# Bias rows for attention: the 16 queries of a set four apart over both halves of the partitions, in two transfers a set

## The chip, the cores and the metric

One core of a Trainium2 chip runs the whole program. The metric is its device time in microseconds; the time of a kernel is the median of its runs. The work is spread over TensorE (PE), VectorE (DVE), ScalarE (ACT), GpSimd (POOL) and the SyncE queue (SP), which here issues every transfer to 16 DMA engines. A profile shows one execution.

## What is computed

Attention with a bias that depends on the positions, and then two feed-forward networks, over B = 4, H = 8, S = 576, D = 64:

```
scores = q @ k.T / sqrt(D)
psi_rel = log1p(abs(i - j));  psi_i = log1p(max(i, 1))
bias[h, i, j] = relu((psi_rel / psi_i) * w1 + b1) @ w2[:, h]      # 32 hidden units
attn = softmax(scores + bias) @ v                                  # 2304 x 512 when laid out
x = max(attn @ w1m, attn @ w2m, attn @ w3m) @ w_out                # hidden width 768
out = g(x @ w_in) @ w_out2                                         # hidden width 2048
```

The bias is the same for all four batches: a table of 8 heads x 576 queries x 576 keys.

## The kernel before, in words

The 576 queries are cut into blocks j = 0 to 3 of 128 queries and a block SJ = 4 of 64. A slot is one head (for SJ, two heads) of one block and one batch. For each slot TensorE makes scores (line 543), VectorE adds the bias and finds the maximum (line 552), ScalarE takes the exponential (line 554) and a 16-bit high half (line 570), GpSimd the low half (lines 571 and 572); the transfer of line 574 transposes both, and TensorE multiplies with v (line 594). In block 0 every other slot is transposed by TensorE. Beside the attention run the first network (lines 649 to 671), whose results go to DRAM (line 678), and the decoding of all weights, which come as 64-bit integers (lines 329, 341 to 344, 155 and 156). The second network (lines 867 and 891) fills the end, from about 700 us.

The bias of a block lies in a table `bias_sb[j]`, [128 queries, 8 heads, 576 keys], which line 552 reads with queries on partitions. It is made in sets of 16 queries, eight sets a block (four for SJ). For a set r, `bias_relu` makes four tiles m (c = 0 to 3). The 128 partitions of a tile hold 4 groups g of 32 hidden units; all groups read one window of the precomputed table `rel`, in which group g is shifted by its own g, and add a column of `tq`. So one tile covers four neighbouring queries, 32j·4 + 16r + 4c + g. `bias_rows` multiplies the tiles with `coef` on TensorE (line 308), which gives 128 rows, row 32c + 8g + h for head h; ScalarE scales each row by a column of `ips` (line 311); and one transfer moves the 128 rows to 16 neighbouring partitions of the table:

```
last_bias[0] = SP.dma_start(bias_sb[j][16 * r:16 * r + 16], t)
```

In block SJ eight small transfers a set, one for each head, do this (line 316).

The eight sets of block 0 are made first, in the order r = 0, 4, 2, 6, 1, 5, 3, 7 (line 725); the loads of lines 730 to 736 are held behind the last of them. The sets of blocks 1 to 3 and SJ are spread over the slots of the block before. The code says in which order work is wanted (priorities, the `sooner` contexts, the counts in `PRM`), and a scheduler that simulates the kernel fixes the order of instructions on each engine when it is built. SP works through its queue in that order: a transfer waits for what it moves, and all behind it wait too.

The last stores are those of line 910, in block SJ two transfers to `out`, whose destination counts 2 batches, 64 rows and 512 columns.

Of the kernel before, what the change touches and what calls it, by code (L numbers as in the profile page):

```python
# [13 lines left out]
ALU = mybir.AluOpType  # L14
# [6 lines left out]
def kernel(ctx: ExitStack, tc: tile.TileContext, qt, kt, vr, small, mw1, mw2, mw3, mwo, win, wo2, out):  # L21
# [7 lines left out]
    V, A, G, T, SP = nc.vector, nc.scalar, nc.gpsimd, nc.tensor, nc.sync  # L29
    P = 128  # L30
    B, H, S, D = 4, 8, 576, 64
# [60 lines left out]
    def st(shape, dt, tag):  # L92
        return sb.tile(shape, dt, tag=tag, name=tag, bufs=BUFS.get(tag, 1))
# [16 lines left out]
    def newcol(n=1):  # L110
        c = col[0]
        col[0] += n
        return vec[:, c:c + n]

    wm = aw.rearrange("p (f i s k c) -> p f i s k c", f=NF1, i=3, s=2, k=KK)
    bias_sb = [ab[:, j % 2].rearrange("p (h k) -> p h k", h=H) for j in range(4)] + [ws[:, 3072:3072 + 4 * S].bitcast(F32).rearrange("p (h k) -> p h k", h=4)]
# [6 lines left out]
    BLK = [(128 * i, 128, 512) for i in range(4)] + [(512, 64, 256)]  # L123
    SJ = 4
# [5 lines left out]
    MAGIC = 12582912.0  # L130
# [31 lines left out]
    if True:  # L162
# [4 lines left out]
        G.memset(ones, 1.0)  # L167
        c_half = newcol()
        G.memset(c_half, 0.5)
        c_g, c_gm, c_p, c_o = newcol(), newcol(), newcol(), newcol()  # L170
        for g in range(4):
            G.memset(c_g[32 * g:32 * g + 32], float(g))
            G.memset(c_gm[32 * g:32 * g + 32], -float(g))


        RW0 = 575
        rel = st([P, 1152], F32, "rel")
        REL = (slice(464, 1152), slice(0, 464))
        pc = st([P, 180], F32, "pc")
        tq, ips = pc[:, 0:144], pc[:, 144:180]  # L180
# [2 lines left out]
        w1c, b1c, w2c = sm[:, 0:1], sm[:, 1:2], sm[:, 2:10]  # L183

        def iota(t, step, n, base, per=0):
            G.iota(t, pattern=[[step, n]], base=base, channel_multiplier=per, allow_small_or_imprecise_dtypes=True)

        iota(rel[:, REL[0]], 1, 688, 464 - RW0)
        iota(tq, 4, 144, 0)
        iota(c_p, 1, 1, 0, 1)  # L190
        iota(ips, 16, 36, 0)
        iota(ident, 1, P, 0, -1)
        iota(rel[:, REL[1]], 1, 464, -RW0)

# [10 lines left out]

        V.tensor_scalar(c_o, c_p, 0.125, -0.4375, ALU.mult, ALU.add)
        V.tensor_scalar(c_o, c_o, MAGIC, None, ALU.add)
        V.tensor_scalar(c_o, c_o, -MAGIC, None, ALU.add)
        V.tensor_scalar(tq, tq, c_g, 1.0, ALU.add, ALU.max)
        V.tensor_scalar(ips, ips, c_o, 1.0, ALU.add, ALU.max)  # L210
        A.activation(rel[:, REL[0]], rel[:, REL[0]], AF.Abs, bias=c_gm)
        A.activation(rel[:, REL[0]], rel[:, REL[0]], AF.Ln, bias=1.0)
        A.activation(pc, pc, AF.Ln, bias=1.0)
# [69 lines left out]
        last_bias = [None, None]  # L283
# [5 lines left out]
        def bias_relu(j, r, engs, tag):  # L289

            ms = []
            for c in range(4):
                x = 32 * j + 4 * r + c
                m = st([P, 9, P], F16, tag).rearrange("p c k -> p (c k)").bitcast(F32) if tag == "pt" else st([P, S], F32, tag)
                win_ = rel[:, RW0 - 4 * x:RW0 - 4 * x + S]
                if engs[c] == "v":
                    V.tensor_scalar(m, win_, tq[:, x:x + 1], 0.0, ALU.add, ALU.max)  # L297
                else:
                    A.activation(m, win_, AF.Relu, bias=tq[:, x:x + 1])
                ms.append(m)  # L300
            return ms

        def bias_rows(j, r, ms, tag):

            pb = ps.tile([P, 2, 512], F32, tag="s", name="s", bufs=2)
            for a in range(2):
                for c in range(4):
                    T.matmul(pb[32 * c:32 * c + 32, a, :288], (coefp if j == SJ else coef), ms[c][:, 288 * a:288 * a + 288], start=True, stop=True)  # L308
            t = st([P, 2 * S], F16, tag).bitcast(F32) if tag == "phl" else st([P, S], F32, tag)
            x = 8 * j + r  # L310
            last_bias[1] = A.activation(halves(t), pb[:, :, :288], AF.Copy, scale=ips[:, x:x + 1])
            if j != SJ:
                last_bias[0] = SP.dma_start(bias_sb[j][16 * r:16 * r + 16], t)
            else:
                for h in range(H):
                    SP.dma_start(bias_sb[j][64 * (h // 4) + 16 * r:64 * (h // 4) + 16 * r + 16, h % 4], t[h:P:8])  # L316


        cnt = {"r": 0, "b": 0}
# [195 lines left out]
        def prefetch(i):  # L515

            if i >= NS:
                return
            u, s = slots[i]
            if u.j == SJ and i + PRM["sa"] < NS:  # L520
                v = slots[i + PRM["sa"]][0]
                load(("q", v.j, v.b, v.x))
            load(("q", u.j, u.b, u.x))
            load(("k", min(u.j, 3), u.b, s if u.j == SJ else s // 2))
# [197 lines left out]
        v_load(0)  # L722
        moe_load(0)
        conv_left = list(range(NF1))
        for x, r in enumerate((0, 4, 2, 6, 1, 5, 3, 7)):
            bias_rows(0, r, bias_relu(0, r, PRM["b0"], ("m", "pt")[x % 2]), ("sp", "phl")[x % 2])
            if x == 1:
                prefetch(1)
        with tc.issue_after(last_bias[0].ins):
            prefetch(2)  # L730
            prefetch(4)
            prefetch(6)
            for ft in range(1, 5):
                moe_load(ft)
                if ft == 2:
                    v_load(1)
# [178 lines left out]
        for x in range(len(work) + GL):  # L915
            if x < len(work):
                y, ft = work[x]
# [9 lines left out]
            if x >= GL:  # L927
                y, ft = work[x - GL]
                size = GROUP if y == 0 else NF2
                g = ft // size if y == 0 else 3 + y  # L930
# [41 lines left out]
```

## Time and profile before

| | |
|---|---|
| median of 3 runs | 1101.57 us (1098.8 to 1102.5) |
| the profiled execution | 1101.92 us |
| its span | 1100.1 us |
| busy: PE, DVE, ACT, POOL | 975.6, 652.2, 562.3, 267.9 us |
| transfers by share of 16 engines | 60.6% of the span |

Busy times are sums over the span, and they don't say which engine ends a stretch. The transfers fill the DMA engines in the first two thirds and hardly appear after; TensorE is busy nearly throughout, and without gaps from 700 us on. A share of the DMA engines over 1 comes from packets that overlap on an engine. [...]

### The profile page before, as it was taken

What the parts mean: (1) busy time and instruction counts of PE and PEld (TensorE: products, weight loads), DVE (VectorE), ACT (ScalarE), POOL (GpSimd) and SP (SyncE); (2) the same over time, 40 slices, a digit from 0 to 9 for tenths busy, and PEclk for the clock granted to TensorE, in tenths of its full rate; (3) what the DMA queues carried; (4) which work ended last, traced back from release to release, by engine and by line L of the source; (5) the groups of instructions that cost most, each with busy time, mean ns of one, the idle gap of its engine ahead of it and who ended that gap; (6) DMA issues with size and microseconds to landing.
All of it is one profiled execution on the core that took longest, in us unless ns stands there. A gap on an engine that the chain in (4) does not pass through costs nothing.

```text
span 1100.1 us, 21901 instructions
## 1 busy us (share of the span) xinstructions
PE 975.6 (89%) x8497; PEld 638.4 (58%) x8497; DVE 652.2 (59%) x1516; ACT 562.3 (51%) x1097; POOL 267.9 (24%) x372
## 2 busy tenths in 40 slices
PE   7457788899899998899899778899999999999994
PEld 4244467676677776677687657644444444444462
DVE  6588784686346773455565587876664454454452
ACT  8685574665465654566676555642332242242341
POOL 0212132554455552635566110100000000000000
PEclk9576698799999998999999999999999999999998
DMA  8997999899999995999999845110020010010010
GB/s 187 267 254 183 243 203 171 178 206 227 214 230 214 217 179 136 224 192 218 183 226 178 206 140 163 58 39 1 1 77 1 1 58 1 1 39 1 1 40 19
DMA packets 233291, 147.84 MB, mean 134 GB/s; under 512 B 177764, under 2 KB 207972, under 8 KB 232676
## 3 DMA queue, kind: packets, MB, share of 16 engines
q1 hardware_dynamic: 233188, 146.45, 60.6%
q8 instruction: 66, 1.08, 0.4%
q14 instruction: 37, 0.30, 0.1%
HBM read 78.65 MB, written 14.68 MB: 85 GB/s over the span
## 4 chain that ended last, share of the span: by engine, by line
PE 55%; DMA 20%; DVE 8%; ACT 6%; issue 4%; SPq 4%; POOL 2%; DVEq 0%; ACTq 0%; POOLq 0%
PE pm L867 17%; PE s L891 17%; PE pm L649 9%; DMA pt<-phl 8%; PE s L543 5%; PE pav L594 3%; PE s L308 2%; DMA v<-in_moe_w_out_dram 2%; DMA ws<-in_moe_w_out_dram 2%; ACT sp L554 2%; SPq L316 1%; DMA x_d<-hl 1%; DMA xT<-phl 1%; POOL phl L572 1%; DVE sp L552 1%
## 5 line engine op out<-in xcount | busy, mean ns | idle before, releaser
L649 PE MATMUL pm<-xT,aw 128*128 128x256 f16 (+1 forms) x2160 | 246.2, 269 | 22.9 <-ACT hm L654 11.3
L649 PEld LDWEIGHTS <-aw 128*128 128x128 f16 x2160 | 193.2, 100 | 70.8 <-issue 47.3
L572 POOL TENSOR_TENSOR phl<-sp,phl 128x512 f16<-128x512 f32 x128 | 157.2, 1228 | 0.0
L543 PE MATMUL s<-k,qz 64*128 64x288 f32 (+1 forms) x576 | 136.5, 472 | 21.2 <-DVE mx L552 17.3
L554 ACT ACTIVATE sp<-sp,mx 128x576 f32<-128x576 f32 x144 | 110.5, 768 | 71.6 <-DVE mx L552 70.7
L891 PEld LDWEIGHTS <-phl 128*128 128x128 f16 x864 | 84.5, 98 | 98.3 <-DVE phl L883 0.2
L552 DVE CUSTOM_DVE_ANT_0 sp<-s,ab 128x576 f32<-128x576 f32 x128 | 93.3, 752 | 53.5 <-PE s L543 30.9
L879 DVE SCALAR_TENSOR_TENSOR sp<-pm,vec,sp 128x512 f32<-128x512 f32 (+1 forms) x80 | 55.8, 697 | 112.7 <-ACT sp L878 112.7
L878 ACT ACTIVATE sp<-pm,vec 128x512 f32<-128x512 f32 (+1 forms) x80 | 58.7, 733 | 123.8 <-PE pm L867 122.2
L891 PE MATMUL s<-ab,phl 128*128 128x512 f16 x486 | 112.5, 379 | 0.0
L882 ACT ACTIVATE phl<-sp,vec 128x512 f16<-128x512 f32 (+1 forms) x80 | 54.3, 678 | 109.5 <-DVE sp L880 109.5
L543 PEld LDWEIGHTS s<-k,qz 64*128 64x128 f32 (+1 forms) x576 | 74.5, 205 | 47.4 <-DVE mx L552 20.7
L570 ACT ACTIVATE phl<-sp 128x576 f16<-128x576 f32 x128 | 85.4, 674 | 28.8 <-DMA pt<-phl 22.9
L571 POOL TENSOR_TENSOR phl<-sp,phl 128x64 f16<-128x64 f32 x128 | 45.4, 355 | 215.1 <-ACT phl L570 202.9
L297 DVE TENSOR_SCALAR m<-rel,pc 128x576 f32<-128x576 f32 x124 | 81.6, 717 | 25.6 <-PE s L308 25.6
L594 PEld LDWEIGHTS <-pt 128*128 128x128 f16 x1792 | 74.5, 101 | 33.7 <-DMA pt<-phl 14.8
L883 DVE SCALAR_TENSOR_TENSOR phl<-sp,vec,phl 128x512 f16<-128x512 f32 (+1 forms) x80 | 55.8, 698 | 51.7 <-ACT phl L882 51.6
L594 PE MATMUL pav<-v,pt 128*128 128x64 f16 x1568 | 70.3, 197 | 17.4 <-DMA pt<-phl 11.4
L671 PE MATMUL pm<-hh,wo 128*128 128x256 f16 x648 | 80.4, 279 | 5.8 <-DVE hm L656 2.5
L867 PEld LDWEIGHTS <-ab 128*128 128x128 f16 x540 | 52.7, 98 | 53.6
L656 DVE SCALAR_TENSOR_TENSOR hm<-pm,hm 128x256 f32<-128x256 f32 (+1 forms) x120 | 47.0, 392 | 47.6 <-PE pm L649 24.5
L671 PEld LDWEIGHTS <-wo 128*128 128x128 f16 x648 | 62.8, 100 | 19.2 <-issue 9.4
(210 smaller groups left out, 1287.3 us busy)
## 6 DMA issues: line engine op xcount, KB each, us to landing
k<-in_k_dram SPq DMA_DIRECT2D x64, 288.0 KB, 4.3
v<-v_d SPq DMA_DIRECT2D x24, 640.0 KB, 5.4
ws<-in_moe_w_out_dram SPq DMA_DIRECT2D x15, 512.0 KB, 5.0
ab<-brow SPq DMA_DIRECT2D x24, 288.0 KB, 6.6
ws<-in_moe_w_in_dram SPq DMA_DIRECT2D x9, 512.0 KB, 5.2
x_d<-hl SPq DMA_DIRECT2D x36, 128.0 KB, 3.2
qz<-in_q_dram SPq DMA_DIRECT2D x16, 256.0 KB, 5.4
qz<-x_d SPq DMA_DIRECT2D x4, 1024.0 KB, 4.8
```

Of the source, the lines that this page charges most:

```text
L297: V.tensor_scalar(m, win_, tq[:, x:x + 1], 0.0, ALU.add, ALU.max)
L543: T.matmul(sbox[i + r][:, c, :288], q[p, s if u.j == SJ else s // 2], k[p, 288 * c:288 * c + 288], start=True, stop=True)
L552: V.tensor_tensor_reduce(halves(sn), sbox.pop(i)[:, :, :288], halves(bias_sb[u.j][:, h]), -0.125, 3e38, ALU.add, ALU.min, mx)
L554: A.activation(pf, sn, AF.Exp, scale=-1.0, bias=mx, accum_out=u.sums[:, h:h + 1])
L570: A.activation(hl[:, :S], pf, AF.Copy)
L572: G.tensor_tensor(hl[:, S + 64:], pf[:, :512], hl[:, :512], ALU.subtract)
L594: T.matmul(u.pav[:, 64 * h:64 * h + 64], pt[:, c], v[:, sl, 64 * (h % 4):64 * (h % 4) + 64], **kw)
L649: T.matmul(o, wm[:, ft, i, wp, kk], x_rhs(key, xp, kk) if n == 256 else x_rhs(key, xp, kk)[:, c], start=(x == 0), stop=(x == 11))
L671: T.matmul(pm, wo16[:, ft, wp, P * d:P * d + P], hh[:, ft, hp], start=(ft == 0 and y == 0), stop=(ft == NF1 - 1 and y == 2))
L867: T.matmul(pm, w[:, wp, kk], x2t[j][:, kk, xp], start=(x == 0), stop=(x == 11))
L878: A.activation(r, pm, AF.Relu, scale=c_ch[:, f], bias=c_half)
L891: T.matmul(acc[c], gl[:, n * gp + P * c:n * gp + P * c + P], w[:, wp], start=(start and y == 0), stop=(stop and y == 2))
```

## The change

A set's 16 queries are now four apart: in the first half of the partitions 32(r // 4) + r % 4 + 4n for n = 0 to 7, and the same 64 further on in the second half. To this end group g of `rel` is shifted by 4g in place of g, the windows start at query i0 of the tile, `tq` and `ips` are numbered accordingly, and each set leaves in two transfers of 64 rows to 8 partitions. In block SJ the 16 queries of a set are four apart over 64 partitions; the number of transfers stays. The sets of block 0 are made in the order 0 to 7, and the load `prefetch(2)`, the second k tile, is asked for after two of them and no longer after the last.

```diff
-        c_g, c_gm, c_p, c_o = newcol(), newcol(), newcol(), newcol()
+        c_g, c_gm, c_p, c_o, c_h, c_oh = (newcol() for _ in range(6))
         for g in range(4):
-            G.memset(c_g[32 * g:32 * g + 32], float(g))
-            G.memset(c_gm[32 * g:32 * g + 32], -float(g))
+            G.memset(c_g[32 * g:32 * g + 32], 4.0 * g)
+            G.memset(c_gm[32 * g:32 * g + 32], -4.0 * g)
+        G.memset(c_h[0:64], 0.0)
+        G.memset(c_h[64:128], 32.0)
...
-        iota(tq, 4, 144, 0)
+        iota(tq, [[16, 36], [1, 4]], None, 0)
...
-        iota(ips, 16, 36, 0)
+        iota(ips[:, 0:32], [[128, 4], [32, 2], [1, 4]], None, 0)
+        iota(ips[:, 32:36], 1, 4, 512)
...
-        V.tensor_scalar(c_o, c_o, -MAGIC, None, ALU.add)
+        V.tensor_scalar(c_o, c_o, -MAGIC, 4.0, ALU.add, ALU.mult)
+        V.tensor_tensor(c_oh, c_o, c_h, ALU.add)
...
-        V.tensor_scalar(ips, ips, c_o, 1.0, ALU.add, ALU.max)
+        V.tensor_scalar(ips[:, 0:32], ips[:, 0:32], c_oh, 1.0, ALU.add, ALU.max)
+        V.tensor_scalar(ips[:, 32:36], ips[:, 32:36], c_o, 1.0, ALU.add, ALU.max)
...
             for c in range(4):
-                x = 32 * j + 4 * r + c
+                i0 = BLK[j][0] + (16 * c + r if j == SJ else 64 * (c // 2) + 16 * (c % 2) + 32 * (r // 4) + r % 4)
+                x = 4 * (i0 // 16) + i0 % 4
...
-                win_ = rel[:, RW0 - 4 * x:RW0 - 4 * x + S]
+                win_ = rel[:, RW0 - i0:RW0 - i0 + S]
...
             if j != SJ:
-                last_bias[0] = SP.dma_start(bias_sb[j][16 * r:16 * r + 16], t)
+                for y in range(2):
+                    i0 = 64 * y + 32 * (r // 4) + r % 4
+                    last_bias[0] = SP.dma_start(bias_sb[j][i0:i0 + 29:4], t[64 * y:64 * y + 64])
             else:
                 for h in range(H):
-                    SP.dma_start(bias_sb[j][64 * (h // 4) + 16 * r:64 * (h // 4) + 16 * r + 16, h % 4], t[h:P:8])
+                    SP.dma_start(bias_sb[j][64 * (h // 4) + r:64 * (h // 4) + r + 61:4, h % 4], t[h:P:8])
...
-        for x, r in enumerate((0, 4, 2, 6, 1, 5, 3, 7)):
+        for x, r in enumerate(range(8)):
             bias_rows(0, r, bias_relu(0, r, PRM["b0"], ("m", "pt")[x % 2]), ("sp", "phl")[x % 2])
             if x == 1:
                 prefetch(1)
+                prefetch(2)
```

The order of the SP queue at the start, before. `hh` are weights of the first network, `ab` is the memory of the bias table, `sp` and `phl` hold a finished set, `aw` takes the next weights.

```order
L329 DMA hh<-in_moe_w_dram 128x4x128 x3
L506 DMA qz<-in_q_dram 128x4x128
L313 DMA ab<-sp 16x8x576
L313 DMA ab<-phl 16x8x576
L313 DMA ab<-sp 16x8x576
L313 DMA ab<-phl 16x8x576
L313 DMA ab<-sp 16x8x576
L313 DMA ab<-phl 16x8x576
L313 DMA ab<-sp 16x8x576
L313 DMA ab<-phl 16x8x576
L509 DMA k<-in_k_dram 128x576 x3
L329 DMA aw<-in_moe_w_dram 128x4x128 x6
```

The same place on SP in the changed kernel, whose lines are numbered 8 higher here.

```order
L337 DMA hh<-in_moe_w_dram 128x4x128 x3
L517 DMA k<-in_k_dram 128x576
L514 DMA qz<-in_q_dram 128x4x128
L321 DMA ab<-sp 8x8x576 x2
L321 DMA ab<-phl 8x8x576 x2
L321 DMA ab<-sp 8x8x576 x2
L321 DMA ab<-phl 8x8x576 x2
L321 DMA ab<-sp 8x8x576 x2
L321 DMA ab<-phl 8x8x576 x2
L321 DMA ab<-sp 8x8x576 x2
L321 DMA ab<-phl 8x8x576 x2
L517 DMA k<-in_k_dram 128x576 x2
```

Each set has two rows of 8 partitions in place of one of 16, and one of the three loads of k has moved ahead of all sets.

The SP queue in block 2, before: the first three loads (line 329) of the second network's weights into `ws` stand among the transposes of its slots.

```order
L506 DMA qz<-in_q_dram 128x4x128
L509 DMA k<-in_k_dram 128x576
L329 DMA ws<-in_moe_w_in_dram 128x4x128
L329 DMA ws<-in_moe_w_out_dram 128x512
L329 DMA ws<-in_moe_w_in_dram 128x4x128
L574 DMA_TRANSPOSE pt<-phl 128x9x128
L313 DMA ab<-brow 16x8x576
```

The SP queue of the changed kernel behind the last small transfers of block SJ, some 130 rows further on.

```order
L517 DMA k<-in_k_dram 128x576
L337 DMA ws<-in_moe_w_in_dram 128x4x128
L582 DMA_TRANSPOSE pt<-phl 128x9x128 x4
L625 DMA_TRANSPOSE xT<-phl 128x8x128
L520 DMA v<-v_d 128x2560
L582 DMA_TRANSPOSE pt<-phl 128x9x128
L337 DMA ws<-in_moe_w_out_dram 128x512
L337 DMA ws<-in_moe_w_in_dram 128x4x128
L582 DMA_TRANSPOSE pt<-phl 128x9x128 x2
```

The three loads are now here; in block 2 none of them is left.

ScalarE before, at the making of block SJ's bias (line 311): two rows of line 342, with three decode steps, read these loads.

```order
L554 ACTIVATE sp,sums<-sp,mx 128x576
L342 ACTIVATE ab<-ws 128x512
L554 ACTIVATE sp,sums<-sp,mx 128x576
L570 ACTIVATE phl<-sp 128x576
L676 ACTIVATE hl<-pm,vec 128x128 x4
L570 ACTIVATE phl<-sp 128x576
L311 ACTIVATE brow<-s,pc 128x576
L676 ACTIVATE hl<-pm,vec 128x128 x2
L311 ACTIVATE brow<-s,pc 128x576
L676 ACTIVATE hl<-pm,vec 128x128 x2
L554 ACTIVATE sp,sums<-sp,mx 128x576
L342 ACTIVATE ab<-ws 128x512 x2
```

ScalarE of the changed kernel, some 30 rows further on, where the first of these steps now stands (line 350).

```order
L668 ACTIVATE hh<-hm 128x256
L562 ACTIVATE sp,sums<-sp,mx 128x576 x2
L578 ACTIVATE phl<-sp 128x576
L662 ACTIVATE hm<-pm 128x256
L578 ACTIVATE phl<-sp 128x576
L350 ACTIVATE ab<-ws 128x512
L616 ACTIVATE phl<-sp 128x512
L349 ACTIVATE sp<-ws 128x512
L562 ACTIVATE sp,sums<-sp,mx 128x576 x2
```

The step has moved from the making of the last bias to the attention of block 3, ahead of exponentials (line 562); the other two follow 13 rows later.

## Rows read from the trace of the kernel before

**Rows 1.** The page: span; busy share of the DMA engines in 40 slices

```profile
span 1100.1 us, 21901 instructions
DMA  8997999899999995999999845110020010010010
```

**Rows 2.** Busy time by stretch, columns in its first row

```profile
core 0: us, PE busy (x) PEld busy (x) DVE busy (x) ACT busy (x) POOL busy (x), PEclk, DMA share, GB/s
20.00:36.00 16.00, 6.61 (x64) 3.29 (x64) 6.78 (x18) 11.45 (x16) 0.00 (x0) 0.75 1.06 120
37.00:40.00 3.00, 0.00 (x0) 0.00 (x0) 0.31 (x1) 0.00 (x0) 0.00 (x0) 0.50 1.06 347
40.00:60.00 20.00, 14.42 (x50) 8.76 (x50) 19.25 (x42) 17.31 (x36) 6.38 (x9) 0.59 1.10 342
80.00:95.00 15.00, 9.93 (x81) 6.01 (x82) 14.88 (x31) 11.07 (x21) 3.97 (x5) 0.70 0.33 92
95.00:400.00 305.00, 275.81 (x3143) 206.99 (x3141) 198.85 (x458) 175.71 (x384) 134.19 (x174) 0.91 1.05 212
700.00:1088.00 388.00, 384.37 (x1931) 188.03 (x1929) 211.54 (x398) 139.99 (x217) 1.15 (x2) 1.00 0.06 20
1090.00:1098.00 8.00, 0.00 (x0) 0.00 (x0) 0.00 (x0) 0.00 (x0) 0.00 (x0) 0.50 0.13 51
```

**Rows 3.** Timeline of the start: start us, us, engine, line, operation, [idle before]

```profile
15.11 0.67 SPq L313 DMA_DIRECT2D ab<-sp  x1
...
25.11 0.55 SPq L313 DMA_DIRECT2D ab<-phl  x1
...
28.34 2.60 ACT L155 ACTIVATE v<-wo,vec 128x1280 f16<-128x1280 f32 x2
30.95 1.28 ACT L554 ACT_TABLE_LOAD   x1
39.69 0.76 DVE L552 CUSTOM_DVE_ANT_0 sp<-s,ab 128x576 f32<-128x576 f32 x1 [11.44 <-DMA k<-in_k_dram]
...
40.49 0.78 ACT L554 ACTIVATE sp<-sp,mx 128x576 f32<-128x576 f32 x1 [8.26 <-DVE mx L552]
```

**Rows 4.** The last set of block 0, from its issue at 25.11 to landing

```profile
DMA to landing us min/median/max: 14.4/14.4/14.4
```

**Rows 5.** Waits at 25 to 50 us: total us, times, longest

```profile
DVE sp L552 <- DMA k<-in_k_dram: 11.4, 1, 11.4
```

**Rows 6.** The 24 later sets, from issue to landing

```profile
DMA to landing us min/median/max: 4.5/6.6/9.9
```

**Rows 7.** DMA issues at 95 to 400 us: count, median us to landing

```profile
pt<-phl SPq DMA_TRANSPOSE x64, 5.7
```

**Rows 8.** The chain of work at 95 to 400 us, shares by line

```profile
by line: PE pm L649 24.2%; PE s L543 14.0%; DMA pt<-phl 12.2%; PE pav L594 7.1%; PE s L308 6.2%; DMA xT<-phl 4.5%; DMA x_d<-hl 3.9%; issue 3.8%; DMA ws<-in_v_dram 2.8%; SPq L574 2.0%; ACT sp L554 1.9%; DVE sp L552 1.4%; ACT phl L570 1.4%; P
```

**Rows 9.** The windows of line 297: duration ns min/median/max, first and last start

```profile
L297 DVE TENSOR_SCALAR m<-rel,pc x124: 420/522/1494, 9.0 to 418.2; 128x576 f32<-128x576 f32 x124
```

**Rows 10.** Timeline of the SP queue: the two places of loads and stores

```profile
232.82 0.43 SPq L329 DMA_DIRECT2D ws<-in_moe_w_in_dram  x1
...
238.83 0.57 SPq L313 DMA_DIRECT2D ab<-brow  x1
...
1085.82 1.35 SPq L910 DMA_DIRECT2D out_dram<-hm  x2
```

**Rows 11.** Who waited for the loads of line 329, 180 to 700 us (us, times)

```profile
  ACT ab L342: 28.9, 13
```

**Rows 12.** Timeline of ACT: where those loads are decoded

```profile
404.65 0.65 ACT L342 ACTIVATE ab<-ws 128x512 uint32<-128x512 uint32 x1
...
471.50 0.67 ACT L342 ACTIVATE ab<-ws 128x512 uint32<-128x512 uint32 x1 [3.39 <-DMA ws<-in_moe_w_out_dram]
```

More of the change, by code (lines that the diff above doesn't have):

```diff
@@ L185, in iota @@
         def iota(t, step, n, base, per=0):
-            G.iota(t, pattern=[[step, n]], base=base, channel_multiplier=per, allow_small_or_imprecise_dtypes=True)
+            G.iota(t, pattern=[[step, n]] if n else step, base=base, channel_multiplier=per, allow_small_or_imprecise_dtypes=True)
         iota(rel[:, REL[0]], 1, 688, 464 - RW0)
-        iota(tq, 4, 144, 0)
+        iota(tq, [[16, 36], [1, 4]], None, 0)
         iota(c_p, 1, 1, 0, 1)
-        iota(ips, 16, 36, 0)
+        iota(ips[:, 0:32], [[128, 4], [32, 2], [1, 4]], None, 0)
+        iota(ips[:, 32:36], 1, 4, 512)
         iota(ident, 1, P, 0, -1)
```

## The prediction, made before the changed kernel ran

> **What bounds the kernel now.** I read the page first, then busy time by stretch, then the timeline of the start, the waits, and the chain of work with its releasers. The profiled execution took 1101.92 us (span 1100.1), 0.35 us above the median of 1101.57, so a sum against it is taken 0.35 lower at the end. From 700 to 1088 us TensorE is busy 384.4 of 388 us and DMA 6% [rows 2]; the change touches nothing there, so that part only starts sooner or later. Before it the DMA engines are full: most of the first 22 slices stand at 9 [rows 1], and from 95 to 400 us, where 24 sets of bias rows leave, their share is 1.05 while TensorE is busy 275.8 of 305 us [rows 2]. Both are near their limit there, and the chain says how often each is last: about 23% of it are transfers (12.2 pt, 4.5 xT, 3.9 x_d, 2.8 ws), the rest mostly TensorE [rows 8].
>
> The start is another matter. Between 28.2 and 39.69 us VectorE sits idle for 11.4 us before the first line 552 [rows 3, 5]. The profile names a load of k, but line 552 reads scores and the bias table, and the last of the eight sets of block 0, issued at 25.11, lands 14.4 us later, at 39.5 [rows 3, 4]. So it waits for the bias. Why does a 288 KB set take so long? From 20 to 36 us, when only these sets are under way, the 16 DMA engines are fully busy (1.06) and move 120 GB/s; from 37 us, with the same busy share and loads that spread over 128 partitions, they move 347 [rows 2]. A set goes to 16 neighbouring partitions. It drains in 294,912 B / 120 GB/s = 2.46 us, and sets are issued every 1.43 us (15.11 to 25.11, seven gaps) [rows 3], so a backlog of some 7 us has grown when the last one is issued.
>
> [...]
>
> **Part 1: eight sets at the start.** No row shows a transfer to partitions four apart, so its pace is bounded: 120 GB/s if the layout is not the cause, 347 if it is and all engines work [rows 2]. Between them lies what the number of engines does. The last two stores go to a destination whose outer dimension counts 2; they run at a DMA share of 0.13, which is 2 of 16 engines, and 51 GB/s, 25 per engine [rows 2, 10]. Each new transfer has 8 partitions outermost, so I take 8 engines, 200 GB/s, and 1.47 us for a set. Both halves then use the same eight, as the two stores together used two.
>
> [...] With 16 engines a set would take 0.85 us.
>
> At 1.47 us against a cadence of 1.43 nearly no queue builds up. The last set lands after its second issue (0.55 us) and a landing like the shortest of the later ones, 4.5 us [rows 3, 6]: 25.11 + 0.55 + 4.5 = 30.2, which is 9.3 sooner. What is last then? ScalarE has its own work until 30.94 and a table load until 32.23, so its first exponential moves from 40.49 to 32.2 at best: 8.3 [rows 3]. The loads that follow in the queue start when the sets are through, near 29 in place of 36.5: 7.5. I take **8 us**, between 0 and 11. It should last: VectorE is busy 19.25 of 20 us from 40 to 60 and 14.88 of 15 from 80 to 95 [rows 2], so what starts sooner there ends sooner. The load of k moved ahead of the sets costs 288 KB at 347 GB/s, 0.85 us, and the same again is gone behind them: nothing, as the queue has gaps before 20 us; uncovered it is 0.85. The two memsets, the extra iota and the two small VectorE steps lie before data that TensorE does not have until the v load lands: nothing, or some tenths of a us.
>
> **Part 2: 24 later sets.** On the busiest engines a set falls from 2.46 to 1.47 us, 24 us in all, 7.5% of the 305 x 1.05 = 320 us of work there [rows 2]; on the other eight all 59 us go, 18%. The transfers on the chain are 23% of 305 us, 71 us [rows 8]. Since a transpose ends with its slowest engine I take the end near 7.5%, 5 us, and add 1 for transposes that stood directly behind a set (median 5.7 us to land [rows 7]): **6 us**, between 0 and the 29 us that TensorE is idle there.
>
> Against it stand 24 more issues on the SP queue, each about 0.57 us [rows 10], 13.7 us in all. Behind each wait a transpose or a load on SP, and behind these the products with v. SP itself is on the chain with 2% [rows 8], which makes 0.3 us; if it were as often last as the transfers, 3. I take **1 us**.
>
> **Part 3: what the scheduler moved.** Before, three loads of the last weights are issued near 233 us [rows 10] and ScalarE decodes them at 404 to 421, unhurried [rows 12]. In the new order all three stand behind the 32 small bias issues, near 450, and the decode steps shortly behind them. Queued behind such a step on ScalarE are the exponentials of the attention. Line 342 waited 28.9 us in 13 cases for its loads, 2.2 each, and 3.4 at 471.5 [rows 11, 12]. Three times 2.2 is 6.6, of which I take half as hidden, since TensorE has other work: **3 us**. The ends are 0, and 3 x 3.4 plus 1.57 MB at 347 GB/s (4.5 us), 15. The order of TensorE and VectorE between 60 and 200 us changes too; I see no row that gives this a sign, and allow 4 us either way.
>
> **Part 4: small ones.** The windows of line 297 now begin at even as well as odd elements; one takes 420 to 522 ns [rows 9], and 0.1 us off half of them would be 7 us on an engine with a third of its time free: nothing, at most 1 us at the start. The 32 small transfers of the last block keep their number: nothing.
>
> **Sum:** -8 - 6 + 1 + 3 = -10, so 1101.9 - 10 = 1091.9, and 0.35 lower for the median: **1091.5 us**.
>
> **The rivals.**
> - *All engines work, and the queue gives more.* If a set spreads over 16 engines (0.85 us), 24 x 1.6 = 39 us of full DMA time go in part 2. With the share then well under 1, transposes land sooner and 20 of the 29 idle us return: -10 - 20 + 3 = -27, 1074.5. For it: DMA is saturated at 1.05. Against it: the stores on two engines. 0.14.
> - *The layout does not do what it should.* The pace stays at 120 GB/s, because the source or the eight engines hold it there. Then parts 1 and 2 give 0, parts 2 and 3 cost 0 to 3: 1102. For it: every set here has the one layout, so no row parts layout from source. Against it: the same busy share carries 347 GB/s elsewhere. 0.12.
> - *Half the engines at the old pace, slower.* If a packet is as slow as before and only eight engines work, a set runs at 60 GB/s, 4.9 us: at the start 8 x 2.45 = 20 us later, in part 2 23% of 59 us = 14: 1135. It decides from 120 GB/s downwards. Against it: 25 GB/s per engine in the last stores, which go to DRAM though. 0.04.
> - *The new order costs more than the start gives, slower.* At 440 to 475 us ScalarE waits the full 15 us for the three late loads, and the 4 us of the other reordering fall on the wrong side, with part 2 giving nothing: -8 + 1 + 15 + 4 = +12, 1113.5. It decides once these waits exceed 3 us with part 2 at nothing, or 9 us with its 6. 0.07.
>
> **How the numbers follow.** The forecast (1084 to 1098) has 0.63. Differences under 0.3%, 3.3 us, count as the same, since a measurement of this kernel can't tell less. Faster: the forecast and the first rival, less a little for the forecast's upper edge, 0.75. Same: the second rival and that edge, 0.14. Slower: the last two, 0.11. The range leaves out half of the first rival and the far ends of the slow ones: 1075 to 1104.
>
> **What would show it.** Right: from 20 to 30 us more than 170 GB/s; the last set of block 0 lands near 30; the first line 552 starts at 30 to 32; at 95 to 400 us the DMA share falls and the whole stretch ends 10 to 14 us sooner. 700 to the end keeps its length. Wrong: sets still at 120 GB/s, or a first line 552 that starts early while the stretch to 95 us has not become shorter, or ScalarE waiting 10 us and more for line 329's loads near 450.

## The result, and the profile after

The changed kernel took 1086.72 us (median of 4 runs, 1084.52 to 1088.28), the kernel before beside it 1100.55: a ratio of 0.9872, 95% interval 0.9846 to 0.9898, or 14 us less. The forecast was 1091.5 (1075 to 1104). The sign and the size are near, but of the four parts of the sum two held; the start gave little and the late loads, booked as a loss, went with a gain. Of all runs below one of `spread_all`, 1190.32 us at a granted clock of 0.79 of full speed, is of the chip's slower state, and the ratios leave it out.

The page of the changed kernel, taken in the fastest of its runs (1084.52 us): span, and the busy share of the DMA engines in 40 slices, which answers [rows 1].

```profile
span 1082.7 us, 21943 instructions
...
DMA  6988887899999987999899644110010010010010
```

Busy time by stretch, changed kernel; columns in the first row. It answers [rows 2].

```profile
core 0: us, PE busy (x) PEld busy (x) DVE busy (x) ACT busy (x) POOL busy (x), PEclk, DMA share, GB/s
20.00:30.00 10.00, 7.71 (x86) 3.54 (x79) 8.34 (x21) 9.09 (x16) 0.00 (x0) 0.98 0.49 163
95.00:400.00 305.00, 284.27 (x3281) 213.56 (x3278) 209.07 (x471) 181.72 (x398) 138.06 (x180) 0.93 0.94 209
691.00:1068.00 377.00, 376.73 (x1861) 181.41 (x1858) 202.49 (x367) 134.92 (x208) 0.00 (x0) 1.00 0.06 20
1070.00:1082.00 12.00, 0.00 (x0) 0.00 (x0) 0.00 (x0) 0.00 (x0) 0.00 (x0) 0.53 0.12 43
```

From 691 us on TensorE is as full as before, so the 17.4 us between the two spans were won ahead of it (between the medians it is 14). From 95 to 400 us the DMA share is 0.94 for 1.05 at nearly the same bytes (209 for 212 GB/s), and TensorE does 284.3 us of work there for 275.8.

The start of the changed kernel: issues of the first and the last set on SP, and the first line 560 (line 552 before) with the wait ahead of it in brackets. It answers [rows 3].

```profile
17.05 1.50 SPq L321 DMA_DIRECT2D ab<-sp  x2
...
28.51 1.63 SPq L321 DMA_DIRECT2D ab<-phl  x2
...
34.66 0.76 DVE L560 CUSTOM_DVE_ANT_0 sp<-s,ab 128x576 f32<-128x576 f32 x1 [4.77 <-DMA ab<-phl]
```

VectorE waits 4.77 us for the last set in place of 11.4, and begins 5.0 us earlier; the prediction's sum took 8.

The chain of work from 95 to 400 us in the changed kernel, shares by line, against [rows 8]:

```profile
by line: PE pm L657 26.4%; PE s L551 13.8%; DMA pt<-phl 7.8%; PE pav L602 7.3%; PE s L314 6.9%; issue 4.5%; PE pm L679 3.9%; DMA ws<-in_moe_w_dram 2.9%; DMA xT<-phl 2.6%; DMA ws<-in_v_dram 2.5%; ACT sp L562 2.2%; DMA x_d<-hl 1.9%; SPq L324 
```

The transposes of pt are last in 7.8% for 12.2%, xT in 2.6 for 4.5, x_d in 1.9 for 3.9. By shares of 305 us that is 13.4, 5.8 and 6.1 us less; loads into `ws` took some of it back (2.9 and 2.5% for 2.8). A share of a chain is no saving: the shares always add up to the whole, and what leaves one line goes to another.

### The profile page after: what moved, and what is told of

Same layout as the page of the kernel before. It is cut to its first block, busy times and chain, and to the rows that moved or that the text cites. A ratio compares the mean times of both kernels' runs of the same rounds, so it can differ in the third digit from the quotient of the medians.

```text
span 1082.7 us, 21943 instructions
## 1 busy us (share of the span) xinstructions
PE 969.9 (90%) x8497; PEld 637.2 (59%) x8497; DVE 657.1 (61%) x1518; ACT 561.5 (52%) x1097; POOL 265.9 (25%) x375
## 4 chain that ended last, share of the span: by engine, by line
PE 62%; DMA 15%; DVE 7%; ACT 7%; issue 4%; SPq 2%; POOL 1%; DVEq 0%; ACTq 0%; POOLq 0%
PE pm L876 17%; PE s L900 17%; PE pm L657 12%; PE s L551 6%; DMA pt<-phl 4%; PE pav L602 3%; PE s L314 3%; DMA ws<-in_moe_w_out_dram 3%; PE pm L679 2%; DMA v<-in_moe_w_out_dram 2%; ACT sp L562 1%; DMA v<-in_moe_w_in_dram 1%; DMA ws<-in_moe_w_in_dram 1%; DMA wo<-in_v_dram 1%; DMA ws<-in_moe_w_dram 1%
## 5 line engine op out<-in xcount | busy, mean ns | idle before, releaser
L657 PE MATMUL pm<-xT,aw 128*128 128x256 f16 (+1 forms) x2160 | 242.8, 266 | 21.9 <-ACT hm L662 6.8
L551 PE MATMUL s<-k,qz 64*128 64x288 f32 (+1 forms) x576 | 134.3, 464 | 15.9 <-DVE mx L560 14.0
L602 PEld LDWEIGHTS <-pt 128*128 128x128 f16 x1792 | 75.0, 102 | 35.9 <-issue 13.4
L669 POOL TENSOR_TENSOR hh<-hm,hh 128x256 f16<-128x256 f32 (+1 forms) x60 | 42.1, 703 | 121.2 <-ACT hh L668 111.2
```

The costliest lines, as they stand in the source:

```text
L551: T.matmul(sbox[i + r][:, c, :288], q[p, s if u.j == SJ else s // 2], k[p, 288 * c:288 * c + 288], start=True, stop=True)
L602: T.matmul(u.pav[:, 64 * h:64 * h + 64], pt[:, c], v[:, sl, 64 * (h % 4):64 * (h % 4) + 64], **kw)
L657: T.matmul(o, wm[:, ft, i, wp, kk], x_rhs(key, xp, kk) if n == 256 else x_rhs(key, xp, kk)[:, c], start=(x == 0), stop=(x == 11))
```

## The experiments

The times are of one chip for each group of runs, and the kernel before moved between groups (1099.5, 1103.6 and 1102.1 us), so the runs are compared by their ratio to it. A change of ratio is turned into us with 1100.55.

### The layout alone, and the cut alone

Three kernels made from the one before, with nothing of the change but what is shown: no new order of sets, no earlier `prefetch(2)`, no new layout in block SJ and, in `spread_all` and `spread_mid`, no new numbering, so that amount and kind of work stay but rows lie at the places of other queries. `spread_all` sends every set of blocks 0 to 3 to the new partitions, `spread_mid` only those of blocks 1 to 3, `near2` cuts the set in two as well but keeps neighbouring partitions.

The edit of `spread_all` (and, where j is not 0, of `spread_mid`):

```diff
-                last_bias[0] = SP.dma_start(bias_sb[j][16 * r:16 * r + 16], t)
+                for y in range(2):
+                    i0 = 64 * y + 32 * (r // 4) + r % 4
+                    last_bias[0] = SP.dma_start(bias_sb[j][i0:i0 + 29:4], t[64 * y:64 * y + 64])
```

That of `near2`:

```diff
-                last_bias[0] = SP.dma_start(bias_sb[j][16 * r:16 * r + 16], t)
+                for y in range(2):
+                    i0 = 16 * r + 8 * y
+                    last_bias[0] = SP.dma_start(bias_sb[j][i0:i0 + 8], t[64 * y:64 * y + 64])
```

> The kernel before, with one edit: in blocks 0 to 3 each set leaves in the two transfers of the change, to partitions four apart in both halves. Nothing else of the change is in it (no new numbering, no earlier load of k, the old order of sets), so the rows of a set land at queries they don't belong to, and the output is not the reference's; the time is that of the same work. The order of the engines stays that of the kernel before but for a few rows. Theory A (the layout of the destination frees DMA time): a median of 1084 to 1090 us, the first line 552 at 33 to 36 us, DMA share at 95 to 400 us near 0.94. Rival B (the new order of the queues and the earlier load give the gain): 1097 to 1103 us. Rival C (the splitting in two gives it): as A.

> As the run before it, but with the new transfers in blocks 1 to 3 alone; the eight sets of block 0 go out as in the kernel before. The output is not the reference's in the same way. Theory A with the gain mostly in the later sets: the first line 552 stays near 39.7 us, the time is 1086 to 1092 us, 4 to 5 us over the run with all sets. If the gain were made at the start, 1096 to 1101 us. Rival B: 1097 to 1103 us.

> The kernel before, each set of blocks 0 to 3 split in two transfers of 8 neighbouring partitions (16 r and 16 r + 8): two transfers and 8 engines, as in the change, with the old neighbouring destination. Theory A: fewer partition groups at a time, a set at 60 GB/s or less, the first line 552 at 50 us or later, the DMA share from 20 to 36 us near 0.5 with about 60 GB/s, and 1115 to 1150 us in all. Rival C (splitting frees eight engines and gives the gain): 1085 to 1100 us. Rival B: 1097 to 1106 us.

| kernel | median us | ratio | 95% interval |
|---|---|---|---|
| spread_all | 1092.64 | 0.9926 | 0.9900 to 0.9953 |
| spread_mid | 1094.88 | 0.9957 | 0.9929 to 0.9984 |
| near2 | 1155.91 | 1.0494 | 1.0434 to 1.0553 |

`near2` and `spread_all` have the same instructions in the same order on every engine; only the partitions that the transfers write differ. So the layout is worth 5.7%, some 62 us, once a set is cut in two. Against the kernel before, both spread kernels gained less than expected for the layout (1084 to 1090 and 1086 to 1092 us). Busy time by stretch, `near2` and then `spread_all`; from 20 to 27 us only sets are under way (columns as above):

```profile
20.00:27.00 7.00, 5.54 (x56) 2.66 (x49) 5.47 (x15) 6.19 (x12) 0.00 (x0) 1.00 0.53 108
95.00:400.00 305.00, 249.85 (x2750) 186.25 (x2748) 177.06 (x413) 158.93 (x350) 112.64 (x151) 0.86 1.01 190
```

```profile
20.00:27.00 7.00, 5.48 (x56) 2.60 (x49) 5.47 (x15) 6.19 (x12) 0.00 (x0) 0.98 0.50 152
95.00:400.00 305.00, 279.64 (x3209) 211.32 (x3212) 203.91 (x464) 177.58 (x390) 131.37 (x175) 0.90 0.94 213
```

In both the transfers of the first sets keep the engines busy to about half (shares of 0.53 and 0.50), and move 108 GB/s to neighbours and 152 to partitions four apart. The 152 need not be a limit of the new layout: `spread_all` issues a set every 1.74 us (14.20 to 26.38 us), which is 169 GB/s, so it takes nearly what comes. `near2` falls behind, and its first maximum starts at 42.03 us, that of `spread_all` at 32.70. From 95 to 400 us `near2` fills the DMA engines (1.01) with 190 GB/s, and TensorE gets 2750 matmuls done where `spread_all` does 3209. That the cut without the layout loses was expected (60 GB/s at the start, 1115 to 1150 us); the rate held up at 108 GB/s, and yet the loss is larger, 1155.91 us. In its chain the transposes of pt are last in 21.5% of that stretch. Why two halves at a share of 0.53 hurt so much more than one transfer at a full one (before: 1.06 and 120 GB/s in [rows 2]) is not settled. `spread_mid` shows that the 24 later sets alone give 4.7 us; the eight at the start add 3.4, which the intervals don't part from nothing. From which wait the 4.7 come its chain does not show: there the transposes of pt are last more often than before, not less (12.2% in [rows 8]):

```profile
by line: PE pm L654 18.8%; DMA pt<-phl 15.3%; PE s L548 10.2%; issue 7.1%; PE s L308 6.4%; PE pav L599 5.5%; PE pm L676 4.4%; DMA ws<-in_v_dram 3.0%; DMA ws<-in_moe_w_out_dram 2.5%; POOL phl L577 2.5%; SPq L579 2.3%; DMA x_d<-hl 2.2%; DVE s
```

### One half, one transfer

`half` is the changed kernel with a set's 16 queries four apart over one half, so that one transfer with 16 partitions outermost takes it (the windows of the tiles and `ips` are numbered to fit); the first sets alternate between the halves.

```diff
-                for y in range(2):
-                    i0 = 64 * y + 32 * (r // 4) + r % 4
-                    last_bias[0] = SP.dma_start(bias_sb[j][i0:i0 + 29:4], t[64 * y:64 * y + 64])
+                i0 = 64 * (r // 4) + r % 4
+                last_bias[0] = SP.dma_start(bias_sb[j][i0:i0 + 61:4], t)
...
-        for x, r in enumerate(range(8)):
+        for x, r in enumerate((0, 4, 1, 5, 2, 6, 3, 7)):
```

> The changed kernel, but the 16 queries of a set lie four apart over one half of the partitions (64 (r // 4) + r % 4 + 4 n), so that a set leaves in one transfer to 16 partitions; the sets of block 0 in the order 0, 4, 1, 5, 2, 6, 3, 7. Numbering of tq and ips follows. Theory A: 16 engines at work, from 20 us on 170 GB/s and more, half the issues on the SP queue, so the first line 552 comes 1 to 3 us sooner than in the changed kernel (34.7), and 1082 to 1088 us in all. Rival C (eight engines left free matter): the DMA share at 95 to 400 us stays over 1.0 and the time is 1089 to 1095 us.

It took 1075.6 us, ratio 0.9796 (0.9758 to 0.9834): by ratio 8 us below the changed kernel, and the intervals do not touch. Both times expected of it (1082 to 1088 and 1089 to 1095) lay higher. Its start, the first and last issue and the first maximum (line 555 here), and from 20 to 30 us:

```profile
14.02 0.63 SPq L316 DMA_DIRECT2D ab<-sp  x1
...
24.09 0.67 SPq L316 DMA_DIRECT2D ab<-phl  x1
...
29.34 0.76 DVE L555 CUSTOM_DVE_ANT_0 sp<-s,ab 128x576 f32<-128x576 f32 x1 [2.13 <-DMA ab<-sp]
```

```profile
20.00:30.00 10.00, 5.69 (x56) 2.75 (x48) 6.38 (x16) 9.22 (x14) 0.00 (x0) 0.98 0.86 241
```

One issue a set goes out faster, the engines are busy to more than half (the share of 0.86 has the loads behind the sets in it from 24.81 us on; from 20 to 24 it is 0.74), and the first maximum comes 10.4 us before that of the kernel before. Two kernels test what of this counts. `half2` cuts the set of `half` in two again, both parts in the one half; `half_o8` makes the first sets in the order 0 to 7, so that four in a row go to the same half, with every engine's order as in `half`. The edit of `half2`:

```diff
-                last_bias[0] = SP.dma_start(bias_sb[j][i0:i0 + 61:4], t)
+                for y in range(2):
+                    last_bias[0] = SP.dma_start(bias_sb[j][i0 + 32 * y:i0 + 32 * y + 29:4], t[64 * y:64 * y + 64])
```

and `half_o8`:

```diff
-        for x, r in enumerate((0, 4, 1, 5, 2, 6, 3, 7)):
+        for x, r in enumerate(range(8)):
```

> The kernel of the run named half (1075.6 us), but each set leaves in two transfers of 8 partitions four apart, 0 to 28 and 32 to 60 of its half. Theory F (what half gains over the changed kernel comes from one issue on the SP queue and 16 engines in place of two and 8): the first line 552 at 32 to 35 us, DMA share from 20 to 30 us near 0.5, and 1084 to 1090 us. Rival G (it comes from the sets lying in one half, or from another order of the engines): 1074 to 1079 us.

> half with the sets of block 0 made in the order 0 to 7, so that the first four all go to the first half and the last four to the second, in place of alternating. Every engine keeps its order. If two sets in a row get in each other's way on one half, the first line 555 starts some us later than half's 29.34 and the ratio rises from 0.980 to over 0.985; if only the spread inside a set counts, it stays at 29 to 30 us and 0.980.

`half2`: 1082.18 us, ratio 0.9798 (0.9764 to 0.9832), its first maximum at 32.43 us, 3 us later than in `half`. `half_o8`: 1077.48 us, 0.9778 (0.9744 to 0.9812), its first maximum at 29.08 us, as early as in `half`. So neither the single issue nor the alternation is needed for the total. What is left is the destination (one half or both) or the order that the scheduler made, for `half2` is ordered otherwise than the changed kernel in some places. Two more kernels exchange only the destinations, without the numbering that goes with them, and keep every engine's order: `after_h` is the changed kernel that writes one half, `half2_b` is `half2` that writes both. The edit of `after_h`:

```diff
-                    i0 = 64 * y + 32 * (r // 4) + r % 4
+                    i0 = 64 * (r // 4) + 32 * y + r % 4
```

That of `half2_b`:

```diff
-                i0 = 64 * (r // 4) + r % 4
+                i0 = 32 * (r // 4) + r % 4
...
-                    last_bias[0] = SP.dma_start(bias_sb[j][i0 + 32 * y:i0 + 32 * y + 29:4], t[64 * y:64 * y + 64])
+                    last_bias[0] = SP.dma_start(bias_sb[j][i0 + 64 * y:i0 + 64 * y + 29:4], t[64 * y:64 * y + 64])
```

> The changed kernel with one edit: the two transfers of a set go to partitions 0 to 28 and 32 to 60 of one half, four apart, in place of one to each half. Every engine keeps its order, and size and number of transfers stay; the rows of blocks 0 to 3 land at wrong queries, so the output is not the reference's. Theory L (a set that lies in one half is written faster than one that is cut over both): about 8 us below the changed kernel, ratio 0.980 to the kernel before, and the lead at slot 24 is over 5 us. Theory O (the lower times of half and half2 come from the engines' order): the same as the changed kernel, 0.987.

> The reverse pair: half2, in its order of engines, with the destination of its two transfers cut over both halves as in the changed kernel; the rows of blocks 0 to 3 land at wrong queries, so the output is not the reference's. Theory L (one half is faster): it loses about 8 us against half2, ratio 0.987 to the kernel before. Theory O (the order): it stays at 0.980.

| order of | written to both halves | to one half |
|---|---|---|
| the changed kernel | 0.9872 (0.9846 to 0.9898) | 0.9852 (0.9817 to 0.9888) |
| half2 | 0.9840 (0.9799 to 0.9881) | 0.9798 (0.9764 to 0.9832) |

Corner to corner the 8 us are real. Each side, 2 to 6 us, lies within the intervals, so both theories keep a share and neither is shown. What falls is that both halves would be better than one by more than some 3 us.

### What the start gives, and the three late loads

`spread_sj` is `spread_all` with block SJ's small transfers four apart as well, and like it without the numbering. `nopf` is the changed kernel without the earlier load of k. The edit of `spread_sj`:

```diff
-                    SP.dma_start(bias_sb[j][64 * (h // 4) + 16 * r:64 * (h // 4) + 16 * r + 16, h % 4], t[h:P:8])
+                    SP.dma_start(bias_sb[j][64 * (h // 4) + r:64 * (h // 4) + r + 61:4, h % 4], t[h:P:8])
```

That of `nopf`:

```diff
             if x == 1:
                 prefetch(1)
-                prefetch(2)
```

> The kernel of the first run (new transfers in blocks 0 to 3, nothing else; 1092.6 us there), and the small transfers of block SJ go to partitions four apart as well. In its order the three late weight loads now stand behind the small transfers of block SJ, as in the changed kernel; the output is not the reference's. Theory D (moving these loads helps, since their traffic leaves block 2): 1085 to 1089 us, the lead over the kernel before grows by 5 us and more between slots 88 and 104. Rival, the prediction's term (ScalarE waits for them, 3 us lost): 1094 to 1098 us. Rival E (only the load of k and the numbering part the first run from the changed kernel): 1091 to 1094 us.

> The changed kernel with the second k tile asked for behind the last set of block 0 again. If the earlier load matters: its transfer comes behind the sets, TensorE's scores for slot 2 wait for it, and the time is 1089 to 1094 us. If it does not: 1084 to 1088 us, the first line 552 at 34 to 35 us or up to 0.9 sooner.

`spread_sj`: 1086.47 us, ratio 0.9840 (0.9800 to 0.9881). `nopf`: 1090.38 us, 0.9877 (0.9841 to 0.9913), the same as the changed kernel. In its page the first set leaves at 15.19 us and the first maximum starts at 32.69, in the page of the changed kernel at 17.05 and 34.66. The earlier load of k is not the reason: the kernel `stores`, described further down, has the changed kernel's order with this load up to its last stores, and its first set leaves just as early, its first maximum starts at 32.65:

```profile
7.39 1.92 SPq L517 DMA_DIRECT2D k<-in_k_dram  x1
...
15.20 1.48 SPq L321 DMA_DIRECT2D ab<-sp  x2
```

What differs is the granted clock. From 13 to 15 us TensorE works on the first bias rows, in the changed kernel after next to no work from 8 to 10.4 (0.02 us busy); the changed kernel, then `stores`:

```profile
13.00:15.00 2.00, 2.00 (x15) 0.62 (x12) 0.00 (x0) 0.00 (x0) 0.00 (x0) 0.50 1.09 352
```

```profile
13.00:15.00 2.00, 2.00 (x27) 0.78 (x26) 1.38 (x4) 1.23 (x2) 0.00 (x0) 1.00 1.14 360
```

At a granted clock of 0.50 it does 15 matmuls there, at 1.00 27. Why the clock fell in the one and not in the other is open. Two executions of one start can thus lie 2 us apart, and the 5.0 us above are known no better than that.

Most of the start's gain is gone again later. The count of finished matmuls shows it (each kernel does 8497 in all): busy time to 95 us, to 160, from there to 404, and to 476. The kernel before:

```profile
0.00:95.00 95.00, 58.28 (x544) 37.54 (x545) 70.41 (x168) 70.59 (x121) 15.62 (x37) 0.76 0.90 218
0.00:160.00 160.00, 110.75 (x1081) 73.42 (x1082) 121.02 (x281) 108.05 (x193) 31.25 (x58) 0.77 0.94 223
160.00:404.00 244.00, 227.34 (x2646) 174.34 (x2646) 150.90 (x352) 140.10 (x316) 120.83 (x156) 0.94 1.06 205
404.00:476.00 72.00, 61.79 (x624) 45.61 (x622) 28.90 (x68) 35.10 (x79) 28.75 (x42) 0.91 0.85 175
```

The changed kernel:

```profile
0.00:95.00 95.00, 60.84 (x539) 40.05 (x540) 72.62 (x169) 70.10 (x120) 14.99 (x42) 0.71 0.81 235
0.00:160.00 160.00, 112.05 (x1081) 75.70 (x1082) 123.78 (x283) 107.63 (x194) 28.46 (x61) 0.77 0.81 227
160.00:404.00 244.00, 236.69 (x2763) 180.35 (x2763) 160.03 (x365) 145.96 (x330) 124.60 (x160) 0.95 0.97 208
404.00:476.00 72.00, 61.61 (x702) 49.49 (x701) 30.69 (x81) 40.26 (x89) 33.13 (x49) 0.98 0.95 208
```

`spread_all`, `spread_mid` and `half`, one fence each:

```profile
0.00:160.00 160.00, 119.91 (x1080) 80.21 (x1081) 122.12 (x274) 107.18 (x192) 29.86 (x58) 0.70 0.79 222
160.00:404.00 244.00, 232.96 (x2704) 177.90 (x2704) 158.91 (x364) 144.86 (x327) 122.03 (x160) 0.94 0.97 212
```

```profile
0.00:160.00 160.00, 114.11 (x1096) 75.50 (x1100) 121.58 (x283) 107.28 (x193) 30.92 (x58) 0.75 0.87 224
```

```profile
0.00:160.00 160.00, 119.32 (x1195) 80.25 (x1195) 127.57 (x297) 112.71 (x206) 34.59 (x63) 0.80 0.89 239
```

At 160 us the changed kernel and `spread_all` have done 1081 and 1080 matmuls, the kernel before 1081, and `spread_mid`, with the old transfers at the start and a first maximum at 37.07 us, 1096: nothing is left of the 5 and 7 us by which the first maximum came sooner. Of the kernels shown only `half` keeps its lead, with 1195. In the chain of work of the changed kernel two waits for loads into `ws` stand out (start, us, what):

```profile
112.47 8.88 DMA ws<-in_moe_w_dram
...
135.19 4.16 DMA ws<-in_moe_w_out_dram
```

In the kernel before the one long wait of this kind is 8.63 us for `in_v`, at 94.97. That such waits end the lead is argued and not shown, and three things speak against it as the whole cause. At 95 us, before either wait, the changed kernel had done 539 matmuls and the kernel before 544. Its ninth maximum starts at 72.5 us (72.1 before), the 13th at 104.9 (112.1), the 17th at 145.6 (146.5), so the lead goes, comes and goes, as it would by another order of work alone. And `half` waits too (10.46 us at 104.22) and keeps its lead. Two rivals stand untested: the new order of TensorE and VectorE between 60 and 160 us, and the clock, which differs between these pages. In `spread_all` 1080 matmuls take TensorE 119.91 us at a granted clock of 0.70, in the kernel before 1081 take 110.75 at 0.77.

From 160 to 404 us the changed kernel does 117 matmuls more than before, `spread_all` 58. The step between `spread_all` and `spread_sj`, 0.9926 to 0.9840 with intervals apart, is 9.5 us (by the intervals some 4 to 15). With it come the new layout in block SJ, and the same move of the three late loads as in the changed kernel: the first leaves at 230.78 us in `spread_all` and at 433.50 in `spread_sj`:

```profile
433.50 0.43 SPq L331 DMA_DIRECT2D ws<-in_moe_w_in_dram  x1
```

So the move, which the prediction charged with 3 us, came together with a gain of 9.5. The two were not parted by a run, and the two pages don't part them either. Matmuls to 230 us, `spread_all` and then `spread_sj`:

```profile
0.00:230.00 230.00, 185.17 (x1823) 130.21 (x1824) 171.16 (x411) 150.56 (x291) 58.47 (x97) 0.74 0.79 209
```

```profile
0.00:230.00 230.00, 179.25 (x1894) 127.63 (x1894) 175.47 (x418) 154.66 (x299) 61.00 (x102) 0.79 0.81 214
```

Up to there both kernels have the same work in the same order, and yet the page of `spread_sj`, its fastest run, is ahead by 71 matmuls, at a granted clock of 0.79 for 0.74. At 404 us, with 3871 for 3784, it is ahead by 87. So only 16 were added where the loads and the layout differ, and the pages say little on the 9.5 us, which rest on the medians. For the layout speaks that the 32 small transfers land sooner in `half` (median 1.9 us) than in the kernel before (2.7); for the move, that 1.57 MB less have to pass full DMA engines (a share of 0.97 from 160 to 404 us in `spread_all`).

### The last stores

The tail was no part of the change, but its rows had served the prediction as a price for few engines [rows 2, 10]. `half_stores` is `half`, and `stores` the changed kernel, with the last stores cut by batch, so that 64 rows are outermost on both sides.

```diff
-                    SP.dma_start(out.rearrange("(b i) d -> b i d", b=B)[c * reps:c * reps + reps, i0:i0 + nr], o)
+                    for x in range(reps):
+                        SP.dma_start(out.rearrange("(b i) d -> b i d", b=B)[c * reps + x, i0:i0 + nr], o[nr * x:nr * x + nr])
```

> The kernel named half, and the last stores of block SJ cut by batch, so that each has 64 rows outermost on both sides in place of 2 and 128. If the number of engines follows the outer sizes: the stores run on 16 engines, the tail behind the last product falls from some 13 us to 5 to 7, and the time to 1066 to 1070 us. If writing to DRAM sets their pace of 51 GB/s: 1074 to 1078 us.

> The changed kernel with the last stores of block SJ cut by batch, so that 64 rows and not 2 batches are their outermost dimension. As the tail of half fell from 14.5 to 5.6 us with this edit, I expect 9 us here too: ratio 0.979 to the kernel before. If other work ends late behind the last product, under 3 us: 0.985.

`half_stores`: 1068.23 us, ratio 0.9685 (0.9650 to 0.9720). `stores`: 1077.71 us, 0.9784 (0.9751 to 0.9817). The last stores of `half`, issued 14.5 us before its span ends at 1071.1:

```profile
1056.61 1.37 SPq L914 DMA_DIRECT2D out_dram<-hm  x2
```

Those of `half_stores`, issued 5.6 us before its end at 1066.9, and the stretch behind them:

```profile
1061.26 2.72 SPq L915 DMA_DIRECT2D out_dram<-hm  x4
```

```profile
1062.00:1064.00 2.00, 0.00 (x0) 0.00 (x0) 0.01 (x1) 0.00 (x0) 0.00 (x0) 1.00 0.59 136
```

A DMA share of 0.59 and 136 GB/s stand where the changed kernel has 0.12 and 43. The edit is worth 9.7 us on the changed kernel and 12 on `half`, by ratios; the tail of `half` itself became 8.9 us shorter. `half_stores` is the fastest of all kernels run, 3.1% below the kernel before.

## Why the prediction came out near

**What bounds the kernel.** Held. The share of the DMA engines fell in the stretch that was called full, and the part from the second network on kept its length: its first product, line 867 before and 876 after, moved from 711.5 to 694.1 us, by the same 17.4 us as the end of the span (the last two times of a row are first and last start).

```profile
L867 PE MATMUL pm<-ws,ab x324: 272/379/379, 711.5 to 1062.7; 128*128 128x512 f16 x108, 128*128 128x256 f16 x54
```

```profile
L876 PE MATMUL pm<-ws,ab x324: 272/379/379, 694.1 to 1045.3; 128*128 128x512 f16 x108, 128*128 128x256 f16 x54
```

**Part 1, 8 us at the start.** Half right at its place, wrong for the whole. The busy time is that of eight engines, as taken from the two stores: a share of 0.49 from 20 to 30 us, where the sign asked for was over 170 GB/s and 163 stand. What failed there is the last landing, at 34.3 us in place of 30.2:

```profile
29.33 5.01 DMA ab<-phl
```

Of these some 4 us, 1.5 lie in the cadence. I kept the 1.43 us between sets of the kernel before; the rows show eight pairs of issues of 1.26 to 1.70 us, one set each 1.64 us on average (17.05 to 28.51). Another 0.3 lie in the second issue (0.82 us after the first, where 0.55 was taken), 0.5 in the landing (5.0 for 4.5), and 1.9 in a first set that left late in this execution, at the lower clock (0.50 from 13 to 15 us), and not behind the load of k. The larger failure is the sentence "It should last". A VectorE that was busy 14.88 of 15 us did not make what lies behind it end sooner: 1081 matmuls at 160 us in both. Why is open, as said above. By the runs the first eight sets give 3.4 us of the total in place of 8, and the intervals don't part that from nothing.

**Part 2, 6 us less 1 for the issues.** Right in size: `spread_mid` gives 4.7 us (1.8 to 7.8). The place, the transposes, is borne out by the chain of the changed kernel (7.8% for 12.2), but not by that of `spread_mid` (15.3%). The 48 issues do not show as a cost on the chain of the whole span, where SP fell from 4% to 2% (before, then after):

```profile
PE 55%; DMA 20%; DVE 8%; ACT 6%; issue 4%; SPq 4%; POOL 2%; DVEq 0%; ACTq 0%; POOLq 0%
```

```profile
PE 62%; DMA 15%; DVE 7%; ACT 7%; issue 4%; SPq 2%; POOL 1%; DVEq 0%; ACTq 0%; POOLq 0%
```

**Part 3, 3 us for the late loads.** The loss did not come. ScalarE does wait for them, as the prediction's last sentence asked for: 11.2 us in five waits between 420 and 480 us of the changed kernel (total us, times, longest),

```profile
ACT ab L350 <- DMA ws<-in_moe_w_in_dram: 5.8, 3, 4.2
ACT ab L350 <- DMA ws<-in_moe_w_out_dram: 5.4, 2, 3.0
```

and yet TensorE does 702 matmuls from 404 to 476 us where it did 624. So by this count the waits of ScalarE there did not hold up the kernel. The step left out the other side of a move, what the loads no longer take from the full stretch they left, and part 4 put the layout of block SJ at nothing because the number of transfers stays. Together these gained 9.5 us, where a loss of 3 was booked; what the move alone does is not shown.

**Part 4, nothing for the windows of line 297.** Right: 521 ns for 522 before [rows 9], and at even and odd starts alike (511 to 519 ns in the third set, 510 to 520 in the fourth).

```profile
L303 DVE TENSOR_SCALAR m<-rel,pc x124: 423/521/1475, 9.9 to 403.5; 128x576 f32<-128x576 f32 x124
```

**The sum.** By the runs: 4.7 for the later sets, 3.4 for the first, 9.5 with block SJ and the loads, and 3.5 us lost with the rest (the order of sets and k; `spread_sj` against the changed kernel, inside the intervals): 14.1. The forecast had 10, with 8 at the start. It came out near by luck: the start's missing 5 us and the 12 by which block SJ and the loads did better lie on opposite sides. **The rivals:** that the layout does nothing, and that half of the engines keep the old pace, fall for this change. `near2` comes out slower still than the second of them (1155.9 us, where 1135 was put), yet not by its mechanism: its transfers move 108 GB/s at a share of 0.53, where the rival gave a set 60. The first rival's time comes with `half`, 1075.6 us for its 1074.5, at a share of 0.74 from 20 to 24 us, but `half2`, with 0.58 from 20 to 30 us (0.86 in `half`) and the same ratio, shows that the higher share at the start is not needed for it.

## What to carry to other kernels

Ask of a transfer into the on-chip memory to which partitions it goes, not only how many: with sets cut in two, rows four apart left at 152 GB/s and neighbouring ones at 108, and one transfer of a set was no worse than two. A gain at the start need not last; count the finished matmuls at a later time before booking it, and compare two executions of one order first, to know what a difference of 2 us at the start or of 71 matmuls at 230 us is worth. When a step is moved out of a stretch, price what the stretch gains by its absence with the same care as what it costs where it arrives.

## What was not expected of the hardware

- At half the share of the engines nearly as much went to neighbouring partitions: 108 GB/s at 0.53 (`near2`) against 120 at 1.06 [rows 2], and to partitions four apart 152 at 0.50 (`spread_all`). At the start of `near2` the limit was thus the destination, not the number of engines; what at the destination sets it no run shows.
- The last two stores of `half`, with a dimension of 2 outermost, ran at a share of 0.13 for 12 us, as 2 of 16 engines would; cut by batch, with 64 there, the four of `half_stores` ran at 0.59, and the tail became 5.6 us for 14.5. The edit made four stores of two as well, so the two shares agree with a number of engines that follows the outer sizes and don't show that it does.
- A transfer with 8 partitions outermost was dearer to issue than one with 16: 0.61 to 1.04 us each for the first sets of the changed kernel, 0.53 to 0.67 in `half`.
